# Adding x(t,c) and x(-t,-c) ahead of stage one in a fused Fourier mixing and gated feed-forward kernel

## The chip, the cores and the metric

The kernel runs on one core of one Trainium2 chip. The metric is the device time of one execution in microseconds. The kernel before took 616.23 us (median of three runs, 616.19 to 616.68).

The core has five engines, each with its own queue of instructions worked in order. PE (TensorE) multiplies matrices: it holds a weight tile of up to 128 rows by 128 columns and streams the other operand's columns through it into PSUM. ACT (ScalarE), DVE (VectorE) and POOL (GpSimd) work on tiles element by element. SP (SyncE) issues DMAs, which 16 DMA engines carry out.

## The reference

The input `x` has 8 batches of 3008 tokens and 256 channels. The kernel computes

```python
X = np.fft.fft(x, axis=1)            # over the 3008 tokens
X = np.fft.fft(X, axis=2).real       # over the 256 channels
g, val = X @ w_gate, X @ w_val       # 256 -> 1536
out = (0.5 * g * (1 + erf(g / sqrt(2)))) * val @ w_out   # 1536 -> 256
```

The real part of the two transforms is a sum over tokens t and channels c of x(t,c) times cos(2 pi (tk/3008 + cl/256)). The cosine is the same for (t,c) and (-t,-c), tokens counted modulo 3008 and channels modulo 256.

## The kernel before, in words

**Folding.** 3008 is 64 x 47. A token is 47 t1 + j; 64 values of t1 and two halves of j (j below 24, and j from 24 on; the 48th is a zero) lie on the 128 partitions, so a tile holds 24 values of j of 256 channels each. `load_x` (line 201) brings them into three tiles `xins`, eight j each. `fold_x` (218) adds and subtracts channel c and channel 256 - c and writes the two halves, 127 elements each, into `xf` as bf16; `singles` (213) copies channels 0 and 128. For batch 0 DVE folds, for the later ones POOL, two j in a call, in slots spread over the main loop two batches ahead (lines 1042 to 1051).

**Stage one** is the transform over t1. `a_step(b, k)` (486) makes two products of 256 columns, for two values of j, with weights `G[:, j, :]`, into a bank of `ps_d`; ACT (in batch 1 sometimes DVE) copies it to `S1`. Twelve such steps make 24 products a batch. `z_write` (505) sends `S1` to HBM, `z_read` (549) brings it back as `Ap` with 96 partitions: (j, and cosine or sine). Batch 0 takes another way: `a_group(J)` (513), six of them, uses the array in four column groups, and one DMA each goes from `S1` to `Ap` directly.

**Stage two** is the transform over j. `b_steps(b, eo, q)` (560) makes, for 32 frequencies and the two folded halves `eo`, a product with 128 columns of `Ap` as weights and 47 columns of a table (`TP`, `TQ`, for frequency 0 `T0P`, `T0Q`) as the other operand: 64 products a batch, eight in a bank. `evac_top` and `evac_rest` copy each bank to `Y`, 1505 frequencies long. `n_turn`, `n_step` and `n_read` prepare one more row from `Ap`, the table copy `TF` and `TB`.

**The feed-forward part** has the channel transform multiplied into its weights once (`gen_w`, line 411, with the tables `CW`, from weights that `load_w` fetches in parts of 256, 256, 512 and 512 columns and `cast_w` turns to bf16, mostly on POOL). A unit (`open_unit`, 647) is one block of 128 hidden channels and up to 512 frequencies; it gives rows for frequencies k and -k. There are 36 units in a batch, 288 in all, the first 12 of a batch with 481 frequencies. PE makes four or five products a unit into `ps_g` and `ps_v`; ACT applies the Gelu (`glp`, `glm`); DVE makes `ev`, `h` for k, and `dv`; POOL makes `h` for -k from `glm` and `dv` once for two units. In the units listed in `SPLIT` one PE product is replaced by work on DVE (`go`), POOL (`go` + `ge`) and ACT (Gelu of `go`, two units later). The second layer's products with `Wo_sb` go in eights at the end of a unit (`STEPS`) into `ps_o`; ACT copies to `osb`, SP stores.

**Order.** All orders are written out by hand: `_InOrder` keeps program order on each engine. The main loop (955 to 1074) runs over units; the tables `a_first`, `reads_first`, `plan`, `extra` say in which unit of a batch the next batch's stage-one and stage-two steps, the folds and the loads stand. `fill` puts stage-two products between a unit's own. In batch 0 the rest of the weights are made in units 0 to 7 (`extra`). `ps_g` has two banks, `ps_v` two tiles of two banks (each for two units), `ps_o` and `ps_d` one bank each. All loads and stores but two go through SP's queue, in order; the program gives DMAs eight semaphores in turn, so that a DMA may wait for the one eight before it.

**The start** (873 to 930) makes the tables with sines on ACT, folds and transforms batch 0, and keeps PE busy with `warm`, 25 products in all whose result nobody reads. `prow` is a row of numbers that `cols_t` turns into columns by products with one column each.

Of the kernel before, what the change touches and what calls it, by code (L numbers as in the profile page):

```python
# [10 lines left out]
BF16 = mybir.dt.bfloat16  # L11
AF = mybir.ActivationFunctionType
# [25 lines left out]
def kernel(  # L38
# [27 lines left out]
    NJ = 48  # L66
    HJ = 24
    KP = 96
# [14 lines left out]
    TP = const_pool.tile([128, 2 * N2], BF16)  # L83
    TQ = const_pool.tile([128, 2 * N2], BF16)
    T0P = const_pool.tile([128, NJ], BF16)
    T0Q = const_pool.tile([128, NJ], BF16)
# [17 lines left out]
    Ap = const_pool.tile([128, NG, C], BF16)  # L104
# [8 lines left out]
    col_b = const_pool.tile([128, 1], FP32)  # L113
    col_c = const_pool.tile([128, 1], FP32)
    col_j = const_pool.tile([128, 1], FP32)
    prow = const_pool.tile([1, 641], BF16)
    cols = const_pool.tile([128, 5], FP32)
    col_w = const_pool.tile([128, 1], FP32)
# [6 lines left out]
    def S1_tile():  # L125
        return work.tile([128, HJ, C], BF16, tag="S1", bufs=1, name="S1")

# [69 lines left out]
    def z_tile():  # L197
        return dram.tile([HJ, 128, C], BF16, tag="z", bufs=2, name="z")


    def load_x(b, i):
        xt = xins[i]
        for o, n, nh in ([(0, 7, 2), (7, 1, 1)] if i == 2 else [(0, 8, 2)]):
            src = ap_replace(
                x, ap=[[N2 * C, N1], [HJ * C, nh], [1, n * C]],
                offset=x.offset + (b * T + 8 * i + o) * C)
            p_step = xt[:, :, :].ap[0][0]
            dst = ap_replace(
                xt[:, :, :], ap=[[p_step * 2 // nh, N1 * nh], [1, n * C]],
                offset=xt[:, :, :].offset + o * C)  # L210
            sync.dma_start(out=dst, in_=src)

    def singles(i, a0=0, an=8):
        pool.tensor_copy(
            _sub(xf, [[C, an], [128, 2]], (8 * i + a0) * C),
            _sub(xins[i], [[C, an], [128, 2]], a0 * C))

    def fold_x(b, i, eng, a0=0, an=8, single=True):
        xt = xins[i]
        o0 = (8 * i + a0) * C  # L220
        lo = _sub(xt, [[C, an], [1, 127]], a0 * C + 1)
        hi = _sub(xt, [[C, an], [-1, 127]], a0 * C + 255)
        ea = _sub(xf, [[C, an], [1, 127]], o0 + 1)
        od = _sub(xf, [[C, an], [1, 127]], o0 + 129)
        eng.tensor_tensor(ea, lo, hi, op=ALU.add)
        eng.tensor_tensor(od, lo, hi, op=ALU.subtract)
        if single:
            singles(i, a0, an)
# [6 lines left out]
    vec.memset(xins[2][:, 7, :], 0.0)  # L235
# [6 lines left out]
    pool.tensor_scalar(rowk, rowk, 1.0 / 64.0, None, op0=ALU.mult)  # L242
# [4 lines left out]
    row = lambda i, pat, off=0: _sub(prow, pat, 128 * i + off, 0, 1)  # L247
    for k in range(2):
        iota(row(0, [[24, 4], [6, 2], [3, 2], [1, 3]], 12 * k), [[1, 4], [0, 2], [4, 2], [8, 3]], 24 * k, 0)
    for i, (base, sign) in enumerate(((0, 1), (0, 1), (1, -1))):  # L250
        iota(row(1 + i, [[12, 8], [6, 2], [1, 6]]), [[0, 8], [sign, 2], [0, 6]], base, 0)
    pool.memset(row(0, [[128, 4], [1, 32]], KP), 0.0)
    pool.memset(row(4, [[1, 129]]), 1.0)

    def cols_t():
        ps = ps_o()
        for i in range(5):
            pe.matmul(ps[:, i : i + 1], _sub(prow, [[1, 128]], 128 * i, 0, 1),
                      _sub(prow, [[1, 1]], 640, 0, 1), start=True, stop=True)
        vec.tensor_copy(cols, ps[:, :5])  # L260
        vec.tensor_scalar(col_j, cols[:, 0:1], 1.0 / N2, None, op0=ALU.mult)
        vec.tensor_scalar(col_w, cols[:, 4:5], -TWO_PI, None, op0=ALU.mult)

    def quats():
        for o, b0 in ((0, 0.25), (N2, 0.0)):
            pool.tensor_scalar(
                _sub(quat, [[1, N2]], o), _sub(cols, [[0, N2]], 1),
                0.25, b0, op0=ALU.mult, op1=ALU.add)
# [4 lines left out]
    def rows_t():  # L273
        pool.tensor_scalar(col_c, col_p, 1.0 / C, None, op0=ALU.mult)
# [6 lines left out]
        iota(_sub(rowt, [[NG, 2], [1, NG]], TG), [[0, 2], [-11, NG]], 0, 0)  # L281
# [20 lines left out]
    vec.memset(zero, 0.0)  # L302
    act.activation(col_m[:, :], zero[:, :], AF.Sin)

# [6 lines left out]
    vec.tensor_scalar(col_a, col_p, 360.0, None, op0=ALU.mult)  # L311
    vec.scalar_tensor_tensor(col_a, col_f, -719.0, col_a, op0=ALU.mult, op1=ALU.add)
    vec.tensor_scalar(rowj, rowj, col_a, None, op0=ALU.add)
    vec.scalar_tensor_tensor(col_b, col_f, -2.0, col_p, op0=ALU.mult, op1=ALU.add)
    vec.tensor_scalar(col_h[1], col_b, -TWO_PI, None, op0=ALU.mult)
    vec.tensor_scalar(col_h[0], col_b, TWO_PI, -TWO_PI, op0=ALU.mult, op1=ALU.add)
# [13 lines left out]
    def phase_g(i):  # L330
        ph, red = pha_g[i // 2][:, i % 2, :], red_g[i // 2][:, i % 2, :]
# [10 lines left out]
        vec.tensor_scalar(cos, cos, 0.25, None, op0=ALU.add)  # L342
        reduce_phase(ph, red)

    def sin_g(i):
        for h in range(2):
            act.activation(
                _sub(G, [[128, 8], [1, 64]], i * 8 * 128 + h * 64),
                _sub(reds[i], [[64, 8], [1, 64]], 0), AF.Sin, scale=col_h[h][:, :])

    def turn_g(odd):
        for to, of, n, sign in (((1, 33, 8, 1.0), (33, 1, 8, -1.0), (3, 35, 8, -1.0), (35, 3, 8, 1.0))
                                if odd else ((0, 0, 16, 1.0), (2, 2, 16, -1.0))):
            pat = [[128, 8], [64, 2], [4, n]]
            to, of = _sub(G, pat, 16 * 128 + to), _sub(G, pat, of)
            if odd:
                act.activation(to, of, AF.Copy, scale=sign)
            else:
                pool.tensor_scalar(to, of, sign, None, op0=ALU.mult)

# [8 lines left out]
    def sin_t(ph, red):  # L369
        s = lambda t, o, n: _sub(t, [[1, n]], o)  # L370
        act.activation(s(ph, 0, 2 * NJ), s(red, TO, 2 * NJ), AF.Sin, scale=col_w)
        for i, t in enumerate((TP, TQ)):
            act.activation(
                _sub(t, [[N2, 2], [1, N2]], 0), _sub(red, [[0, 2], [1, N2]], i * N2), AF.Sin, scale=col_w)
        act.activation(_sub(TB, [[1, 2 * NG]], 0), s(red, TG, 2 * NG), AF.Sin, scale=col_w)
        for i, t in enumerate((T0P, T0Q)):
            pool.tensor_scalar(
                t[:, :MID], s(ph, i * NJ, MID), cols[:, 3:4], None, op0=ALU.mult)
            pool.tensor_scalar(
                t[:, MID:], s(ph, i * NJ + MID, MID), cols[:, 2:3], None, op0=ALU.mult)  # L380
# [3 lines left out]
    def phase_c():  # L384
        both = red2_tile()
        redc.append(both)
        for q, (o, n) in enumerate(((0, 129), (129, 127))):
            act.activation(both[:, o : o + n], rowc[:, o : o + n], AF.Copy, scale=col_c[:, :],
                           bias=0.25 * (q + 1))

    def reduce_c():
        reduce_phase(redc[0][:, :C], redc[0][:, C : 2 * C])

    def sin_c():
        act.activation(_sub(CW, [[1, C]], 0), redc[0][:, C : 2 * C], AF.Sin, scale=-TWO_PI)
# [709 lines left out]
```

## Time and profile before

| | us | share |
|---|---|---|
| time of the profiled execution | 616.14 | |
| its span, first to last instruction | 614.30 | |
| PE matmul busy | 597.6 | 97% |
| DVE busy | 567.2 | 92% |
| POOL busy | 501.5 | 82% |
| ACT busy | 487.4 | 79% |
| a batch of the main loop (batches 1 to 5) | 72.3 to 72.4 | |
| granted PE clock, over the span | 1.00 | |

Busy time is the time in which an engine had at least one instruction at work. The products are pipelined: the mean of a group is from a product's start to its modelled end, longer than what it costs in a row of many; the cost is the distance between starts, which the chain shows as a time for so many products. The page's groups name the output and input tiles, the shapes, the count, the busy time, the mean in ns, and the idle time of the engine before them with what ended it. Nearly all instructions carry line 25, the helper that issues them, so tiles and shapes tell them apart.

### The profile page before, as it was taken

Reading aid. Unit: us, or ns where it says so; the run is one execution under the profiler, and the core shown is the slowest. Engines: PE = TensorE matmul, PEld = TensorE weight load, DVE = VectorE, ACT = ScalarE, POOL = GpSimd, SP = SyncE. Lnnn points to the kernel's source line nnn. Section 1 sums busy time; section 2 is a strip of 40 time slices with the busy share of each in tenths; the row PEclk is TensorE's granted clock in tenths of the full one; section 3 lists DMA queues with packets and bytes.
Section 4 is the critical chain, followed back from the end, with each engine's and each line's share of the span. In section 5 each row is a group of like instructions: output and inputs, shape, how many; then the busy total and the mean of one; then the engine's idle time right before and its main releaser. Section 6 shows DMA issues by size and latency. Waiting matters only on the chain.

```text
span 614.3 us, 13104 instructions
## 1 busy us (share of the span) xinstructions
PE 597.6 (97%) x4581; PEld 399.8 (65%) x4638; DVE 567.2 (92%) x689; ACT 487.4 (79%) x1011; POOL 501.5 (82%) x525
## 2 busy tenths in 40 slices
PE   4999999999999999999999999999999999999997
PEld 2556666666676666666667666766667666666666
DVE  8788999999999999999999999999999999999992
ACT  8798789877898787977789778887789878776762
POOL 5599999989999899798998899898997755665552
PEclk9999999999999999999999999999999999999999
DMA  7989424772257612674246633476223712222123
GB/s 277 348 233 264 135 65 116 202 216 60 61 149 197 197 39 70 205 224 113 66 120 173 192 93 74 121 207 209 46 67 100 203 37 52 59 47 52 39 48 86
DMA packets 63459, 80.79 MB, mean 132 GB/s; under 512 B 8186, under 2 KB 56826, under 8 KB 60674
## 3 DMA queue, kind: packets, MB, share of 16 engines
q1 hardware_dynamic: 61682, 79.05, 45.5%
q0 software_dynamic: 1552, 0.79, 0.9%
q8 instruction: 36, 0.59, 0.4%
q14 instruction: 29, 0.24, 0.1%
q10 hardware_dynamic: 160, 0.13, 0.1%
HBM read 43.47 MB, written 35.68 MB: 129 GB/s over the span
## 4 chain that ended last, share of the span: by engine, by line
PE 91%; ACT 3%; DMA 2%; DVE 2%; SPq 1%; issue 1%; ACTq 0%; POOL 0%
PE ps_o L25 38%; PE ps_g L25 26%; PE ps_v L25 20%; PE ps_d L25 7%; DMA xin<-in_x_dram 1%; ACT glm L25 1%; ACT osb L25 1%; ACT S L25 1%; SPq L850 1%; DMA out_dram<-osb 1%; ACT glp L25 0%; DVE h L25 0%; SPq L855 0%; DVE red L25 0%; DVE ev L25 0%
## 5 line engine op out<-in xcount | busy, mean ns | idle before, releaser
L25 POOL TENSOR_TENSOR h<-glm,dv 128x1024 bf16<-128x1024 bf16 (+1 forms) x138 | 290.8, 2109 | 80.6 <-DVE dv L25 60.0
L25 PE MATMUL ps_o<-Wo_sb,h 128*128 128x256 bf16 x2124 | 284.2, 272 | 1.0
L25 PEld LDWEIGHTS <-h 128*128 128x128 bf16 x2208 | 211.0, 98 | 58.3 <-issue 0.9
L25 DVE SCALAR_TENSOR_TENSOR ev<-nq,WN,ps_v 128x512 f32<-128x512 bf16 (+1 forms) x276 | 202.2, 734 | 23.4 <-PE ps_v L25 13.4
L25 ACT ACTIVATE glp<-ps_g 128x512 bf16<-128x512 f32 (+1 forms) x288 | 169.8, 590 | 37.2 <-PE ps_v L25 18.6
L25 ACT ACTIVATE glm<-ps_g 128x512 bf16<-128x512 f32 (+1 forms) x241 | 142.2, 590 | 56.6 <-PE ps_g L25 44.0
L25 DVE TENSOR_TENSOR h<-glp,ps_v 128x1024 bf16<-128x1024 bf16 (+2 forms) x150 | 173.0, 1154 | 4.2 <-ACT glp L25 3.5
L25 DVE SCALAR_TENSOR_TENSOR dv<-ev,ps_v 128x1024 f32<-128x1024 f32 (+1 forms) x138 | 164.9, 1195 | 0.0
L25 POOL TENSOR_TENSOR xf<-xin 128x254 bf16<-128x254 f32 x168 | 118.1, 724 | 0.4 <-PE ps_g L25 0.4
L25 PE MATMUL ps_v<-Y,WOP 128*128 128x512 bf16 (+1 forms) x288 | 107.7, 374 | 0.1
L25 PE MATMUL ps_v<-Y,WE 128*128 128x512 bf16 (+1 forms) x286 | 107.3, 375 | 0.0
L25 PE MATMUL ps_g<-Y,WE 128*128 128x512 bf16 (+1 forms) x266 | 99.3, 373 | 0.0
L25 PE MATMUL ps_g<-Y,WOP 128*128 128x512 bf16 (+1 forms) x257 | 96.0, 373 | 0.8
L25 PE MATMUL ps_g<-Y,WOM 128*128 128x512 bf16 (+1 forms) x241 | 90.3, 375 | 0.2
L25 PEld LDWEIGHTS <-WOP 128*128 128x128 bf16 x576 | 55.5, 97 | 49.2 <-ACT WOP L25 0.6
L25 PEld LDWEIGHTS <-WE 128*128 128x128 bf16 x576 | 56.0, 97 | 27.8 <-issue 2.0
L25 ACT ACTIVATE osb<-ps_o 128x512 f32<-128x512 f32 x92 | 54.2, 589 | 13.4 <-PE ps_o L25 11.9
L25 POOL TENSOR_TENSOR go<-go,ge 128x480 f32<-128x480 f32 (+1 forms) x47 | 58.1, 1236 | 7.1 <-DVE go L25 7.1
L25 PEld LDWEIGHTS <-Ap 96*128 96x128 bf16 (+1 forms) x561 | 39.6, 96 | 31.7 <-issue 0.2
L25 ACT ACTIVATE S<-ps_d 128x512 bf16<-128x512 f32 x82 | 48.9, 596 | 0.2 <-PE ps_d L25 0.2
L25 PEld LDWEIGHTS <-G 128*128 128x128 bf16 (+1 forms) x289 | 22.0, 110 | 26.5 <-issue 4.7
L25 DVE SCALAR_TENSOR_TENSOR go<-nq,WN,ps_g 128x480 f32<-128x480 bf16 (+1 forms) x47 | 34.3, 730 | 2.6 <-ACT glp L25 1.9
(134 smaller groups left out, 371.8 us busy)
## 6 DMA issues: line engine op xcount, KB each, us to landing
out_dram<-osb SPq DMA_DIRECT2D x358, 64.0 KB
xin<-in_x_dram SPq DMA_DIRECT2D x16, 1024.0 KB
Ap<-z SPq DMA_DIRECT2D x20, 512.0 KB
xin<-in_x_dram SPq DMA_DIRECT2D x8, 896.0 KB
z<-S SPq DMA_DIRECT2D x7, 768.0 KB
z<-S SPq DMA_DIRECT2D x6, 512.0 KB
nq<-nrow SPq DMA_DIRECT2D x8, 376.2 KB
z<-S SPq DMA_DIRECT2D x9, 256.0 KB
```

Of the source, the lines that this page charges most:

```text
L25: return lambda *a, **k: self._tc.keep_in_program_order(call(*a, **k))
L850: queues[q % 2].dma_start(out=rows_ap(rows[0][0], 32, rows[1][0] - rows[0][0], 2), in_=_sub(t, [[C, 2], [1, C]], 0, 32 * q, 32))
```

## The change

The pair x(t,c) + x(-t,-c) is added before stage one, so that stage one has 12 values of j instead of 24 for each half.

- For a reversed token the order of t1 turns round on the partitions, which a load alone would take in single rows. `flip(b)` copies the needed tokens of `x` within HBM to `xr`, reversed, in two DMAs of 11 x 64 and 12 x 64 rows of 1 KB. `flip(1)` stands between the second and third pair of weight loads, `flip(2)` in unit 4 of batch 0, the later ones at unit 24, three batches ahead.
- `load_x` becomes four DMAs (`put_x`), each to every second partition: two from `x`, two from `xr`. In batch 0 it is three, all from `x`.
- `fold_part` replaces `fold_x` on POOL, in halves of two j: the first adds channels 0 and 128 and adds the reversed partner to 254 channels of two j in place, in float32; the second folds as before. There are 12 halves a batch, with their own unit tables (`folds`), where there were 12 calls. Batch 1's stand in units 3 to 14 of batch 0 instead of 0 to 11.
- `a_step` uses the weights `GA`, made from `G` by `gen_ga` (two ACT instructions in unit 8 of batch 0), six steps of two products a batch, all in `ps_d` and copied by ACT; `z`, `S1` and `Ap` halve.
- In stage two, a column block of `Ap` serves two frequencies: 32 products of 94 columns, `TPQ` with three groups of 94 columns in place of four tables. `fill` puts one product at a time where it put two.
- Batch 0 isn't added ahead; `a_group` runs its six groups with 16 products of 128 columns each, keeping of each folded half only the cosine or sine part, so that its `Ap` has the new layout.
- At the start 12 rows of `prow` are made instead of five, ACT clears them first, and the phases of `G` and `CW` are reduced as integers with one bitwise and instead of two float32 operations. `gen_tf` has seven POOL instructions instead of three, in unit 17 instead of 13. `STEPS`, `SPLIT` and `warm` are as they were.

```diff
+    def flip(b):
+        xr[b] = xr_tile()
+        for s, (j0, n) in enumerate(((N2 - HP + 1, HP - 1), (HP, HP))):
+            d = xr[b][s, :, :, :]
+            sync.dma_start(
+                out=ap_replace(d, ap=[[C, n], [HP * C, N1], [1, C]], offset=d.offset),
+                in_=ap_replace(x, ap=[[C, n], [-N2 * C, N1], [1, C]],
+                               offset=x.offset + (b * T + N2 * (N1 - 1) + j0) * C))
...
+        put_x(i, 0, 0, 4, xb(j, [[C, 4]]))
+        put_x(i, 1, 0, 4, xb(N2 - HP - j, [[-C, 4]]))
+        put_x(i, 0, 5 - o, 3 + o, xv(0, HP - 2 + o - j, [[-C, 3 + o]]))
+        put_x(i, 1, 4, 4, xv(1, j, [[C, 4]]))
...
+    def fold_part(b, i, k):
+        a0 = k // 2 * 2
+        o0 = (HP * (b % 2) + 4 * i + a0) * C
+        at = lambda s, o, pat: _sub(xins[i], [[C, 2]] + pat, (s + a0) * C + o)
+        if k % 2 == 0:
+            pool.tensor_tensor(
+                _sub(xf, [[C, 2], [128, 2]], o0), at(0, 0, [[128, 2]]), at(4, 0, [[128, 2]]), op=ALU.add)
+            pool.tensor_tensor(
+                at(0, 1, [[128, 2], [1, 127]]), at(0, 1, [[128, 2], [1, 127]]),
+                at(4, 255, [[-128, 2], [-1, 127]]), op=ALU.add)
+        else:
+            for o, op in ((1, ALU.add), (129, ALU.subtract)):
+                pool.tensor_tensor(
+                    _sub(xf, [[C, 2], [1, 127]], o0 + o), at(0, 1, [[1, 127]]),
+                    at(0, 255, [[-1, 127]]), op=op)
...
+        ps = ps_d()
         for i in range(2):
-            jj = 2 * k + i
-            on_half(ps, pe.matmul(
-                ps[:, i * C : (i + 1) * C], G[:, jj, :], _sub(xf, [[1, C]], jj * C),
-                start=True, stop=True))
...
+            pe.matmul(
+                ps[:, i * C : (i + 1) * C], GA[:, 2 * k + i, :],
+                _sub(xf, [[1, C]], (HP * (b % 2) + 2 * k + i) * C), start=True, stop=True)
+        act.activation(_sub(S1, [[1, 2 * C]], 2 * k * C), ps, AF.Copy)
...
-                g = 8 * q + gi
+                g = 4 * q + gi
...
+                t = TPQ[0 if m1 else eo]
+                o = gi * TS
                 r = slice(0, 1) if m1 else slice(0, 128)
+                pat, off = ([[2 * TS, 2], [1, N2]], 0) if g == 0 else ([[TS, 2], [1, N2]], TS + 36 * g % N2)
+                keep(pe.matmul(ps[r, o : o + TS], w, _sub(t, pat, off, 0, KP), start=True, stop=True))
...
     def gen_tf():
-        for i, t in enumerate((TP, TQ, T0P)):
-            pool.tensor_copy(TF[:, i, :], t[:, :NJ])
+        for i, t in enumerate(TPQ):
+            pool.tensor_tensor(TF[:, i, :], t[:, 1, :NJ], t[:, 2, :NJ], op=ALU.add)
+        pool.tensor_copy(TF[:, 2, :], TPQ[0][:, 0, :NJ])
+        for k in range(4):
+            v = _sub(TB, [[1, GH]], k * GH)
+            pool.tensor_scalar(v, v, cols[:, 2 + k : 3 + k], None, op0=ALU.mult)
...
     for f0, n in ((256, 256), (512, 512)):
         for i in (1, 0):
             load_w(f0, i, n)
+        if n == 256:
+            flip(1)
+    pool.memset(xins[0][:, 4, :], 0.0)
     load_x(1, 0)
...
-    extra = {1: [lambda: cast_w(1024)], 2: [lambda: turn_g(False)], 13: [gen_tf]}
+    extra = {1: [lambda: cast_w(1024)], 2: [lambda: turn_g(False)], 8: [gen_ga], 17: [gen_tf]}
...
+    a_first = {9: 0, 10: 1, 11: 2, 12: 3, 14: 4, 16: 5}
+    a_later = {2 * k: k for k in range(HP // 2)}
+    folds = ((16, 18, 19, 21, 22, 24, 26, 27, 29, 30, 32, 34), (5, 7, 9, 11, 19, 21, 23, 25, 29, 31, 33, 35))
+    reads = ({12: 0, 15: 1, 18: 2}, {4: 0, 8: 1, 13: 2})
...
-        def fill(most=2):
+        def fill(most=1):
...
-                if i < 12:
-                    fold_x(1, i // 4, pool, i % 4 * 2, 2)
...
+                if 3 <= i < 15:
+                    fold_part(1, (i - 3) // 4, (i - 3) % 4)
+            if b + 2 < B and i in folds[b > 0]:
+                fold_part(b + 2, *divmod(folds[b > 0].index(i), 4))
```

More of the change, by code (lines that the diff above doesn't have):

```diff
@@ L67 @@
     HJ = 24
+    HP = HJ // 2
     KP = 96
@@ L949 @@
         for h in range(2):
[L950 to L952 removed]
+            later[i0 + h] = [(1, q, 2 * h, 2 * h + 2)]
+    first = {23: ["n"], 22: [(1, 0, 0, 4)]} | {
+        23 + q: [(1, q, 0, 4)] for q in range(1, 4)}
     plan = [first | evens, later | evens]
```

356 lines of the change are left out of this document (173 added, 183 removed).

## The prediction

> **What bounds the kernel now.** I read the page's engine totals, then the chain that ended last, then the busy time stage by stage, then the timeline around the waits. The totals and the chain:
>
> ```profile
> PE 597.6 (97%) x4581; PEld 399.8 (65%) x4638; DVE 567.2 (92%) x689; ACT 487.4 (79%) x1011; POOL 501.5 (82%) x525
> ...
> PE 91%; ACT 3%; DMA 2%; DVE 2%; SPq 1%; issue 1%; ACTq 0%; POOL 0%
> ```
>
> TensorE holds the end almost alone, so its time removed is time saved until DVE (92%) takes over. Batch 3, cut into units 0–11 (stage one of the next batch inside), 12–17 (neither) and 18–35 (stage two inside); columns are window, length, PE, PEld, DVE, ACT, POOL, clock, DMA share, GB/s:
>
> ```profile
> 242.80:266.90 24.10, 24.05 (x174) 16.86 (x174) 22.76 (x28) 21.10 (x41) 20.63 (x21) 1.00 0.64 183
> 266.90:279.10 12.20, 12.15 (x89) 7.97 (x89) 11.63 (x14) 9.22 (x16) 10.38 (x11) 1.00 0.66 201
> 279.10:315.60 36.50, 36.23 (x293) 24.36 (x297) 35.01 (x41) 29.24 (x67) 34.22 (x36) 1.00 0.32 84
> ```
>
> PE idles 0.37 of 72.80 us; DVE idles 1.34, 0.57 and 1.49: 3.4 in all. That is the room. How close DVE follows is in the timeline: `dv` ends, frees its bank of `ps_v`, and PE writes into it 0.26 us later (308.74 to 309.00).
>
> ```profile
> 307.52 1.22 DVE L25 SCALAR_TENSOR_TENSOR dv<-ev,ps_v 128x1024 f32<-128x1024 f32 x1
> 309.00 0.38 PE L25 MATMUL ps_v<-Y,WE 128*128 128x512 bf16 x1
> ```
>
> Batch 0 differs: from the first `h<-glm,dv` on, POOL is as full as PE (second line), and before it the DMAs are busy at 0.88 (first line).
>
> ```profile
> 27.90:54.80 26.90, 26.44 (x189) 14.81 (x191) 22.89 (x37) 24.21 (x49) 25.26 (x49) 1.00 0.88 252
> 54.80:103.80 49.00, 48.63 (x380) 32.23 (x384) 47.21 (x54) 39.85 (x88) 48.61 (x53) 1.00 0.48 137
> ```
>
> Prices: from the chain, 16 stage-two products and 8 of 256 columns; from the groups by form, the folds and POOL's f32 adds.
>
> ```profile
> 21.50 0.41 PE ps_g L25 x16
> 48.29 0.87 PE ps_o L25 x8
> L25 POOL TENSOR_TENSOR xf<-xin 128x254 bf16<-128x254 f32 x168 | 118.1, 724 | 0.4 <-PE ps_g L25 0.4
> L25 POOL CAST xf<-xin 128x4 bf16<-128x4 f32 x84 | 16.9, 202 | 0.0
> L25 POOL TENSOR_TENSOR go<-go,ge 128x512 f32<-128x512 f32 x22 | 28.0, 1272 | 0.0
> ```
>
> **The change part by part.** The sum is made against the profiled execution, 616.14 us (span 614.30 and 1.84 around it), 0.09 under the median of 616.23.
>
> Batches 1 to 6, PE. Stage one loses 12 of 24 products of 256 columns: 12 x 0.87/8 = 1.31 us a batch. Stage two goes from 64 products of 47 columns (0.41/16 = 0.026 each, 1.64) to 32 of 94. Their price lies between 0.026 and twice that; on the line through 0.026 at 47 and 0.109 at 256 columns it is 0.044, so 1.42: 0.2 saved (0 to 0.8). PE: 1.5 us a batch (1.3 to 2.1).
>
> By the Trainium skill (TensorE: Matmul & The Clock Gate, Back-to-back issue gap) a stream of weight loads and products of 128 columns keeps some 81 ns apiece, though alone a product takes N/2.4 + 2.5 ns. By the 81, stage two would cost about 2.6 us and the batch would gain only 0.35; by the other formula 94 columns take 42 ns. The chain's rows, each with its own weight load, agree with the second.
>
> Do DVE and POOL follow? DVE's work per batch stays at 69.4 of 72.8; it would have 71.3. Where PE waits on a bank freed only 0.26 us before, DVE's idle time is half its own echo. In units 0–11, 1.31 goes from PE and DVE has 1.34 to give. I take 1.3 a batch; bounds 0.5 (only a third of DVE's idle time is usable) and 2.1 (all of PE's). POOL: a fold pair was 2 x (two of 0.68, start to start, and a cast of 0.15) = 3.0; now a half A (4-element add 0.15, f32 add of 508 elements, by the 512-element `go` 1.22 apart) of 1.37 and a half B (two of 0.68) of 1.36: 16.4 instead of 18.1 a batch; it needs no more than it frees. ACT loses 6 copies `S<-ps_d` (0.596) and gains two small `Y` copies; off the path. Steady part: 6 x 1.3 = -7.8 (-3 to -12.6).
>
> Data. `z` halves; the flip adds 1.5 MB read and written a batch, each load becomes four. At unit 24 the flip stands on SP ahead of output stores and, through the rotating DMA semaphores, of the eighth DMA after it. `osb` has two buffers and a pair every 6 us, so a store may be some 6 us late; the cover is that spare buffer. Without it ACT's `osb` copy would wait, then `ps_o`. Nothing taken; up to +1 a batch in rival 3.
>
> The start, to 21 us. POOL writes 12 `prow` rows for 5 (0.43 each, +3.0), behind ACT's zeroing of 1408 elements (by 1.02 for 1024, about 1.3); `cols` and with it the second fold on DVE come up to 1.2 late. Against it: DVE drops three range reductions (2 x 0.69, 0.43), stage-two products fall from 99 to 51. The filler matmuls `warm` stay and cover part. +0.3 (-0.5 to +1.3).
>
> The flip of batch 1 is issued ahead of the 512-column weight loads.
>
> ```profile
> 24.04 1.04 POOL L25 CAST wb<-wst 128x1024 bf16<-128x1024 f32 x1 [1.51 <-DMA wst<-in_moe_w_val_dram]
> 28.43 0.38 PE L25 MATMUL ps_o<-wb,CW 128*128 128x512 bf16 x1
> q1 hardware_dynamic: 61682, 79.05, 45.5%
> ```
>
> The cast waits for its load already; its product comes 3.35 us after the cast's end. The flip's time: no row shows HBM to HBM. Lower end 1.5 MB at the 335 GB/s of the stretch 20 to 40 us, 4.5 us; upper end twice the mean rate's 5.3 us (79.05 MB in 45.5% of 16 engines' 614 us is 283 GB/s), as both sides are HBM: 10.6. I take 7, near the middle, since both rows have one HBM side. The load slips by 7, PE waits 7 - 3.35, less 0.4 because the last `Ap<-S` ahead of it is 128 KB smaller (at 335 GB/s): +3.3 (0.8 to 7). The loads of 1024 slip too, inside this.
>
> The Trainium skill (DMA: Bandwidth & Descriptors, Why a DMA increments its semaphore by 16 and not by 1) says that a copy runs on the largest number up to 16 that divides both sides' outermost counts; the flip's are 11 and 12. That is 128 packets in a row on some engines, about 7.4 us by the mean rate; no trace here shows such a split.
>
> Batch 0, PE and POOL. By unit 13 six stage-one steps (0.22 each) are gone or moved behind: -1.3. POOL then: up to the `go` add at 88.98 (unit 31) the new order holds 11 halves (15.0) where 8 pairs of 1.51 stood (12.1), because batch 1's folds start at unit 3 and batch 2's follow at 16; `gen_tf`, formerly done before 54.8, is now 7 instructions, about 1.9. That add comes 4.8 later.
>
> ```profile
> 88.98 1.26 POOL L25 TENSOR_TENSOR go<-go,ge 128x512 f32<-128x512 f32 x1
> 91.09 0.62 ACT L25 ACTIVATE glm<-go 128x512 bf16<-128x512 f32 x1
> ```
>
> ACT read it 0.85 after its end. ACT works in order: behind this Gelu stand `glm` and `glp` of the next units, which free `ps_g` for PE. So 4.8 - 0.85 = 3.9 late, less what ACT's gaps give back: +3.2 (0, if ACT's 9.2 idle us of 49 absorb it, to 4.8). PE doesn't regain it.
>
> Sum: 616.1 - 7.8 + 0.3 + 3.3 - 1.3 + 3.2 = 613.8 us.
>
> **Rivals.** (1) Batch 0 hides both: the flip runs at the lower end and POOL's lag stays inside ACT's gaps. For it: no wait on `go` in batch 0 costs anything now. Against: POOL has 0.4 us idle in 49. With all of PE's 1.5 a batch, 616.1 - 9 - 1.3 + 0.3 + 0.8 = 607. (2) DVE becomes the bound: 0.5 a batch; for it the 0.26 us, against it 3.4 us idle. 613.8 + 4.8 = 618.6. (3) Slower: the flip holds the weights back. One transfer, in units 2 to 7 of batch 0. With the rest as forecast it decides against the change from a wait of 5.6 us, a flip of 9.3; at its upper end 10.6 it waits 7 and gives 617.5; if flips at unit 24 cost 1 us in each of 5 batches too, 622. (4) The weight loads show: a load of `Ap` lasts 97 ns by its group, and if 94 columns don't hide it as the chain's rows say 47 do, 32 of them take 3.1 us and a batch gains nothing: 613.8 + 7.8 = 621.6; the row of 16 in 0.41 speaks against. (By the 81 ns of the Trainium skill's page named above, 0.35 a batch, it would be 619.5.) (5) It doesn't cut what it says: the built program has 84 products of 256 columns in stage one for 168 in the loop, 256 wide ones in stage two for 512, so this is all but excluded.
>
> **How the numbers follow.** Forecast 0.50, (1) 0.20, (2) 0.08, (3) 0.16, (4) 0.03, other mishaps 0.03. Around 613.8 the two batch-0 terms spread 610 to 617.5, the likeliest case's own range. Over all 606 to 619.5 leaves about 2 in 10 out. A difference of 0.2% (1.2 us) is about what can be told. Faster: 0.33 of the forecast's 0.50, 0.20 of (1), 0.03 elsewhere: 0.56. Same: 0.12 of the forecast, 0.02 elsewhere: 0.14. Slower: 0.30.
>
> **What would show it.** Right: `ps_d<-xf,GA` 84 times at 0.109 apart; 94-column products some 0.044 apart; batches 1 to 6 about 71.1 us each with DVE idle near 2; a wait of POOL's 1024-element cast on `wst` past 30 us and of PE behind it; ACT's `glm<-go` waiting for POOL in batch 0, at most 4 us. Wrong: a steady batch over 72 us (DVE or POOL bound), or no wait at all ahead of 104 us (then 607), or `osb` waiting for `out_dram` at each unit 24.

## The result, and the profile after

The changed kernel takes 620.74 us (median, 620.14 to 621.82) against 616.21: 1.0074 times as long, 95% interval 1.0057 to 1.0092. It is slower by 4.5 us; 613.8 was predicted, with a range of 606.0 to 619.5. The profiled execution took 620.70 us, its span 618.6, 4.3 over that of before.

The busy times by stage, cut at the second product of unit 0 (`ps_v<-Y,WOP`, which marks the start of a unit) and of units 36, 252 and 287: the start, batch 0, batches 1 to 6, batch 7, the end. First the kernel before, then the changed one; the columns are window, length, PE, PEld, DVE, ACT, POOL, clock, DMA share, GB/s.

```profile
0.00:24.75 24.75, 15.63 (x236) 9.85 (x238) 19.59 (x55) 19.07 (x48) 11.07 (x40) 1.00 0.87 291
24.75:97.97 73.22, 72.39 (x541) 44.46 (x548) 66.38 (x88) 61.76 (x132) 70.77 (x99) 1.00 0.63 184
97.97:531.88 433.91, 431.63 (x3262) 292.00 (x3303) 415.02 (x475) 356.47 (x744) 377.25 (x364) 1.00 0.46 128
```

```profile
0.00:29.36 29.36, 18.81 (x195) 10.10 (x197) 19.29 (x64) 18.52 (x49) 12.94 (x44) 1.00 0.74 232
29.36:108.24 78.88, 71.86 (x497) 42.98 (x504) 64.74 (x85) 61.93 (x134) 69.14 (x81) 1.00 0.68 203
108.24:536.21 427.97, 425.52 (x3004) 283.42 (x3039) 413.73 (x474) 342.08 (x720) 369.24 (x303) 1.00 0.44 122
```

The steady part gains 5.94 us, the start loses 4.61, batch 0 loses 5.66; batch 7 and the end together gain 0.05. In batch 0 PE is busy 0.5 us less and idle 7.0 instead of 0.8.

**The start.** The timeline of PE in the changed kernel, with the fillers `ps_d<-G`:

```profile
17.95 0.59 PE L26 MATMUL ps_d<-G 128*128 128x512 bf16 x1 [0.85 <-ACT S L26]
18.76 3.62 PE L26 MATMUL ps_d<-G 128*128 128x512 bf16 x8 [0.22 <-issue]
22.17 0.57 PE L26 MATMUL ps_g<-wb,CW 128*128 128x256 bf16 x2
23.23 2.97 PE L26 MATMUL ps_d<-G 128*128 128x512 bf16 x13
26.04 0.34 PE L26 MATMUL ps_v<-tab,Ap 96*128 96x94 bf16 x4
```

Eight products of 512 columns last 3.62 us here, and 4.5 us later thirteen of them last 2.97: they start 0.427 and 0.216 us apart. In the kernel before nine took 2.33:

```profile
14.75 2.33 PE L25 MATMUL ps_d<-G 128*128 128x512 bf16 x9
```

PE's array runs at half rate until about 22.4 us; before, it had reached the full rate by 15.2. The folds come late as well: DVE's first at 8.34 for 6.47, the last ends at 16.55 for 13.83.

**Batch 0.** The waits of PE in its timeline, then the rows of POOL and of SP's queue around the third and the fourth:

```profile
38.93 0.59 PE L26 MATMUL ps_o<-wb,CW 128*128 128x512 bf16 x2 [1.11 <-POOL wb L26]
49.10 0.39 PE L26 MATMUL ps_d<-xf,GA 128*128 128x256 bf16 x2 [0.59 <-ACT GA L26]
64.18 0.38 PE L26 MATMUL ps_d<-xf,GA 128*128 128x256 bf16 x2 [2.12 <-POOL xf L26]
77.27 0.21 PE L26 MATMUL ps_d<-tab,Ap 96*128 96x94 bf16 x2 [1.74 <-issue]
```

```profile
60.61 2.15 POOL L26 TENSOR_TENSOR h<-glm,dv 128x1024 bf16<-128x1024 bf16 x1 [2.56 <-DVE dv L26]
62.72 1.40 POOL L26 TENSOR_TENSOR xf<-xin 128x254 bf16<-128x254 f32 x2
```

```profile
70.03 1.27 SPq L26 DMA_DIRECT2D xin<-in_x_dram  x2
71.35 1.27 SPq L26 DMA_DIRECT2D xin<-xr  x2
72.66 0.59 SPq L26 DMA_DIRECT2D Ap<-z  x1
```

The first wait is for the weights of 1024 columns on. Their load stands on SP behind a load that waits for the copy; the chain shows the copy's second DMA and then this load:

```profile
21.48 8.57 DMA xr<-in_x_dram
30.66 7.12 DMA wst<-in_moe_w_val_dram
```

At 64.18 PE waits for the last half fold of batch 1, which stands on POOL behind an `h` that itself waited 2.56 us for DVE. At 77.27 it waits for the last third of `Ap`, whose read stands on SP behind four loads of `x`.

**The steady part.** Batch 3 of the changed kernel, units 0–11, 12–17 and 18–35, and two groups by form:

```profile
251.21:274.17 22.96, 22.91 (x162) 15.70 (x162) 22.50 (x28) 18.42 (x36) 19.70 (x17) 1.00 0.52 145
274.17:286.46 12.29, 12.24 (x84) 7.87 (x84) 11.69 (x14) 9.10 (x16) 10.65 (x10) 1.00 0.54 158
286.46:322.88 36.42, 36.20 (x265) 24.20 (x268) 35.06 (x41) 29.59 (x69) 33.36 (x29) 1.00 0.43 124
```

```profile
L26 PE MATMUL ps_d<-xf,GA 128*128 128x256 bf16 x84 | 16.0, 272 | 2.7 <-POOL xf L26 2.1 <-ACT GA L26 0.6
L26 PE MATMUL ps_d<-tab,Ap 96*128 96x94 bf16 x228 | 43.2, 206 | 2.2 <-issue 1.7
```

DVE idles 0.46 us in units 0–11, where it idled 1.34. Products of 94 columns start 0.042 us apart. PE idles little in these rows, yet by the starts of its products against their prices it waits, in the mean of batches 1, 3 and 5, 0.09, 0.16 and 0.15 us in units 0, 6 and 12 ahead of a product into `ps_v` (0.01 or less before the change); in batches 2, 4 and 6 it is 0.26, 0.20 and 0.15 (0.04 or less before). Such a wait is shorter than the modelled end of a product and so does not show as idle.

### The profile page after: what moved, and what is told of

Same layout as the page of the kernel before. It is cut to its first block, busy times and chain, and to the rows that moved or that the text cites. A ratio compares the mean times of both kernels' runs of the same rounds, so it can differ in the third digit from the quotient of the medians.

```text
span 618.6 us, 12413 instructions
## 1 busy us (share of the span) xinstructions
PE 594.2 (96%) x4238; PEld 390.1 (63%) x4289; DVE 564.1 (91%) x695; ACT 472.7 (76%) x989; POOL 493.8 (80%) x450
## 4 chain that ended last, share of the span: by engine, by line
PE 83%; DMA 5%; DVE 3%; POOL 3%; ACT 2%; issue 2%; SPq 2%; ACTq 0%; DVEq 0%; POOLq 0%
PE ps_o L26 36%; PE ps_g L26 25%; PE ps_v L26 18%; PE ps_d L26 4%; DMA xr<-in_x_dram 1%; POOL h L26 1%; DMA xin<-in_x_dram 1%; SPq L26 1%; DMA wst<-in_moe_w_val_dram 1%; DVE h L26 1%; DVE dv L26 1%; POOL xf L26 1%; ACT osb L26 1%; DMA xin<-xr 1%; DMA z<-S 1%
## 5 line engine op out<-in xcount | busy, mean ns | idle before, releaser
L26 PE MATMUL ps_g<-Y,WOP 128*128 128x512 bf16 (+1 forms) x271 | 101.3, 374 | 1.4
L26 PE MATMUL ps_g<-Y,WE 128*128 128x512 bf16 (+1 forms) x258 | 96.3, 373 | 0.5 <-ACT glm L26 0.5
L26 POOL TENSOR_TENSOR xf<-xin 128x254 bf16<-128x254 f32 (+1 forms) x126 | 68.6, 562 | 0.4
L26 POOL TENSOR_TENSOR xin<-xin 128x508 f32<-128x508 f32 x42 | 53.4, 1271 | 0.0
L26 PE MATMUL ps_d<-tab,Ap 96*128 96x94 bf16 (+2 forms) x246 | 43.6, 204 | 2.2 <-issue 1.7
L26 ACT ACTIVATE Y<-ps_d 128x192 bf16<-128x192 f32 (+5 forms) x156 | 38.7, 380 | 0.3 <-PE ps_d L26 0.3
```

The source lines that it names most:

```text
L26: return lambda *a, **k: self._tc.keep_in_program_order(call(*a, **k))
```

## The experiments

Edits are against the changed kernel or the one named. Times are medians, ratios those to the kernel before. "Unit 0" is its start as defined above. Unit 0, batch lengths and all lines are those of the one profiled execution of a kernel, which lies up to 3.3 us from the median where a kernel's times scatter.

### The start: clock or loads

`warm_early`:

```diff
     for i in (1, 0):
         load_w(0, i, 256)
+    ps = ps_d()
+    for _ in range(24):
+        pe.matmul(ps, _sub(zero, [[0, 128]], 0), _sub(zero, [[0, 512]], 0), start=True, stop=True)
```

> 24 products of 512 columns of a tile of zeros are put ahead of everything else on PE, from about 1.2 us. In the changed kernel the filler products between 18.8 and 22.2 us start 0.427 us apart, and those from 23.2 us on 0.216 apart. Theory A (PE's own clock: less work in the start leaves the array at half rate until 22 us): the fillers then stand 0.216 apart from the first on, the first product of the channel weights (22.17) comes near 20.3, unit 0 some 2 us earlier, the time near 618.5. Theory B (the late loads alone set the start, the slow fillers only fill a wait): unit 0 stays within 0.5 us of 29.4 and the time at 620.7.

622.04 us, 1.0096 (1.0066 to 1.0125). Unit 0 starts 1.1 us earlier, at 28.28, in a profiled execution of 620.11 us, the second shortest of six (619.55 to 624.93); the median does not follow. The rate rises between 6.7 and 7.0 us (products from 0.427 to 0.219 apart) and is lost again; the windows show it:

```profile
12.00:14.00 2.00, 0.96 (x32) 0.79 (x32) 1.71 (x4) 0.08 (x1) 1.77 (x4) 0.92 1.05 326
14.00:16.00 2.00, 1.55 (x31) 0.68 (x23) 2.00 (x6) 1.30 (x4) 0.75 (x2) 0.50 0.46 100
```

Between 10.9 and 13.5 us PE mostly waits for folds. So neither A nor B as written: the fillers were still slow when they ran. `clock_fill` has the 24 products of `warm_early` and fills that stretch too. (These added products are "the fillers" from here on, those of `warm` the old ones.)

```diff
...
-        if n == 1:
-            warm(2)
+        if n in (1, 3):
+            warm((6, 2)[n // 2])
...
-    warm(WF[0])
+    warm(WF[0], bank=ps_g)
```

> As warm_early, where PE's clock rose at 6.7 us (products of zeros from 0.427 to 0.219 us apart) and had fallen again by 13.8, after a stretch in which PE waited for the folds. Now six fillers instead of two stand behind group 1, two more behind group 3, and the ten behind group 5 go to a bank of ps_g, so that they need not wait for ACT's copies of ps_d. Theory A2 (the clock falls because the halved products of stage one leave PE idle between the folds): fillers stand 0.216 apart from 7 us on, the first product of the channel weights comes at 19.2 to 19.6 (the cast ahead of it ends at 19.2) instead of 22.17, and unit 0 starts at 26.4 to 27; batch 0 then gives some of it back, since the wait at 76.6 to 77.3 us comes at a fixed time in all runs so far: 618 to 619. Rival: the clock falls all the same (more fillers only push the work back): unit 0 at 28.3 or later.

```profile
11.05 1.47 PE L26 MATMUL ps_d<-G 128*128 128x512 bf16 x6
16.49 2.33 PE L26 MATMUL ps_g<-G 128*128 128x512 bf16 x10
18.66 0.38 PE L26 MATMUL ps_g<-wb,CW 128*128 128x256 bf16 x2
```

A2 holds for the start: ten fillers in 2.33 us, the channel weights 3.5 us earlier, unit 0 at 25.67 instead of 29.36. So between these two executions 3.7 of the start's 4.6 us are the clock; 0.9 is left. The time is not the 618 to 619 forecast but 622.2 us, 1.0089 (1.0066 to 1.0112), in ten executions from 619.29 to 625.46. The profiled one is the longest of them, and its batch 0 takes 87.31. PE's largest waits there, what the cast waited for, and a window after the second wait:

```profile
33.14 0.59 PE L26 MATMUL ps_o<-wb,CW 128*128 128x512 bf16 x2 [3.62 <-POOL wb L26]
36.33 1.06 PE L26 MATMUL ps_o<-wb,CW 128*128 128x512 bf16 x2
```

```profile
32.04 1.04 POOL L26 CAST wb<-wst 128x1024 bf16<-128x1024 f32 x1 [9.14 <-DMA wst<-in_moe_w_val_dram]
```

```profile
80.00:82.00 2.00, 2.00 (x10) 1.09 (x8) 0.14 (x1) 1.15 (x6) 2.00 (x3) 0.50 0.00 0
```

The wait that the prediction put down to the copy is now there, 3.62 us for the 512 column weights. And a wait of this size costs twice: after it, and after one of 3.56 us in unit 21, PE runs at half rate for 3 and 6 us.

`asc_first` and `act_queue` ask why the first loads are late.

```diff
-            put_x(i, 1, 4, 4, xb(N2 - HP - j, [[-C, 4]]))
-            put_x(i, 1, 1 - o, 3 + o, xb(N2 - 1 + o - j, [[-C, 3 + o]]))
+            put_x(i, 1, 4, 4, xb(N2 - HP - j - 3, [[C, 4]]))
+            put_x(i, 1, 1 - o, 3 + o, xb(N2 - 3 - j, [[C, 3 + o]]))
```

> The reversed half of batch 0 is read in ascending order of tokens, so that four rows of 1 KB lie side by side; the tokens are then the wrong ones for the reversed half, and nothing else differs. Theory B (the first loads are late because of their rows of 1 KB in descending order): the first fold starts near 6.6 us instead of 8.34, as in the kernel before (6.47), the folds end 1.5 to 2 us earlier and unit 0 starts 1.5 to 2 us earlier: near 619. Rival C (they are late because nine issues of 0.65 us stand on SP's queue where four stood): the first fold stays within 0.4 us of 8.34 and the time within 0.5 us of 620.7. Theory A (clock) says nothing of the loads; if PE is still cold, less than the full gain arrives.

```diff
...
-            put_x(i, 1, 4, 4, xb(N2 - HP - j, [[-C, 4]]))
+            put_x(i, 1, 4, 4, xb(N2 - HP - j, [[-C, 4]]), act if i else sync)
```

> Two of batch 0's nine loads, one each of parts 1 and 2, are issued on ACT's queue ahead of its first table load, so that SP issues seven. Theory C (issues on SP's queue space the loads): the last fold ends 1 to 1.3 us earlier than 16.55, near 15.4, though ACT's phases and G come 1.2 later; unit 0 up to 1 us earlier. Rival H (the rate of the DMA engines with these rows of 1 KB): the last fold stays at 16.3 to 16.6 and the first fold comes later than 8.3, because the early data now stand ahead of part 0's; time 620 to 622.

DVE's folds with ascending rows:

```profile
6.98 2.44 DVE L26 TENSOR_TENSOR xf<-xin 128x1016 bf16<-128x1016 f32 x3 [0.49 <-DMA xin<-in_x_dram]
11.13 2.46 DVE L26 TENSOR_TENSOR xf<-xin 128x1016 bf16<-128x1016 f32 x3 [1.11 <-DMA xin<-in_x_dram]
13.90 2.65 DVE L26 TENSOR_TENSOR xf<-xin 128x508 bf16<-128x508 f32 x6 [0.32 <-DMA xin<-in_x_dram]
```

The first fold comes 1.4 us earlier, the last ends at 16.55 all the same, and the time is 620.12 (1.0056). PE's rate rises no sooner for it: products of 512 columns still start 0.427 us apart at 23.4. With fewer issues on SP the first comes at 8.38 and the last ends at 16.37: 622.6 us (1.0094). So the descending rows explain part 0's delay and neither explains the later parts. What holds these back stays open; by the difference of the two starts above it is worth at most 0.9 us.

### Batch 0: which wait, and what stands behind it

`no_flip`: `flip` is not called, and `xv` in `load_x` reads `x`.

```diff
         xv = lambda s, k, pat: ap_replace(
-            xr[b][s, :, :, :], ap=[[HP * C, N1]] + pat + [[1, C]],
-            offset=xr[b][s, :, :, :].offset + k * C)
+            x, ap=[[N2 * C, N1]] + pat + [[1, C]], offset=x.offset + (b * T + HP * s + k) * C)
...
```

> No copy in HBM is made: the loads of batches 1 to 7 read unreversed rows of x itself where they read the copy, in the same shapes; so the reversed tokens are wrong ones, and 10.5 MB of reading and writing and fourteen issues on SP are gone. The prediction's flip term (the 512 column weights late, PE waiting): PE's waits ahead of 48 us go (1.1 us), and the time falls by 1 to 1.5 us, to about 619.4. Rival F (the flips cost in every batch, through SP's queue and the DMA engines): also 0.3 to 1 us in each of batches 1 to 4, near 616 to 618. Rival G (the flip is hidden anyway): within 0.5 us of 620.7.

620.72 us, 1.0065 (1.0043 to 1.0088): rival G by the time. PE's wait for the weights goes, and unit 4 is 1.3 us shorter; the waits in units 15 and 21 stay (1.90 and 2.35). Behind the second PE falls to half rate, which it did not in the profiled execution of the changed kernel, and unit 21 is 2.0 us longer. So this time does not show that the copy costs nothing.

`fold_early` (first line) and `fold_z` (both):

```diff
-                if 3 <= i < 15:
-                    fold_part(1, (i - 3) // 4, (i - 3) % 4)
+                if 2 <= i < 14:
+                    fold_part(1, (i - 2) // 4, (i - 2) % 4)
...
-            loads = (0, 14, 19) if b else (8, 12, 18)
+            loads = (0, 14, 19) if b else (8, 12, 20)
```

> The twelve half folds of batch 1 stand in units 2 to 13 of batch 0 instead of 3 to 14, so that the last half comes ahead of POOL's first h instead of behind it. Theory D (PE's waits of 2.12 us at 64.2 and of 1.74 us at 77.3 both come from that last half: the first directly, the second because z and Ap of batch 1 follow from it): both go and the time falls by 3.5 to 3.9 us, to about 617. Theory D2 (the second wait is SP's: the read of the last third of Ap stands behind four loads of x on its queue): only the first goes, about 618.6. Rival E (POOL's total is too large in batch 0): the wait comes back at another h or go, and the time stays within 0.6 us of 620.7.

> As fold_early, and in batch 0 the last load of x for batch 2 stands in unit 20 instead of 18, so behind the read of the last third of Ap on SP's queue. Theory D2 (PE's wait in unit 21 is for that read, which stands behind four loads of x; fold_early's gain of 2 us was lost there, where its wait grew from 1.7 to 4.2): the wait in unit 21 falls to under 0.5 us, batch 0 takes 75 to 76 us instead of 78.9, and the time is 616.5 to 617.5. Rival E2 (the DMA engines are full in this stretch, the order on the queue is nothing): the wait in unit 21 stays over 2 us, the time over 619.

`fold_early` takes 622.42 us (1.0093, 1.007 to 1.0115). The wait for the fold is gone and the one for `Ap` has grown to 4.16 us, ending at 76.92 instead of 77.27:

```profile
76.92 0.24 PE L26 MATMUL ps_d<-tab,Ap 96*128 96x94 bf16 x2 [4.16 <-issue]
```

None of the three expectations: the 2.1 us saved are waited away there, 2.4 more than before, and behind a wait of this length PE runs at half rate until some 81 us (a clock of 0.50 in the windows from 76 to 80 us). With the load of `x` behind the read of `Ap`, `fold_z` has no wait in unit 21, batch 0 takes 76.75 us, and the time is 618.36 (1.0032, 1.0015 to 1.005), 0.9 above the range forecast. D2 is right on the cause; 1.31 us come back one unit later, where PE waits for POOL's `NA`, the product of `Ap` and `TB`.

### The steady part

`ev_short`:

```diff
+        if r["kd"] and r["c0"] == 1024 and r["k"]:
+            return
...
-                d["dv"][:, :, :nm], d["ev"][:, :, :nm], 2.0, d["pv"][:, :, :nm],
-                op0=ALU.mult, op1=ALU.subtract))
+                d["dv"][:, :, :nm], _sub(d["ev"][:, :, :], [[512 * (r["c0"] != 1024), 2], [1, nm]], 0),
+                2.0, d["pv"][:, :, :nm], op0=ALU.mult, op1=ALU.subtract))
```

> In the first 12 units of each batch after the first, DVE's ev of every second unit is left out and dv takes the other unit's ev twice, so part of the output is wrong: DVE has 6 x 0.7 = 4.2 us less to do in each of those stretches and PE the same. Theory J (what the steady part fell short by, 1.0 us a batch for the 1.3 forecast, is PE waiting 0.09, 0.16 and 0.15 us in units 0, 6 and 12 for DVE to free ps_v): these waits go and a batch takes 0.3 to 0.45 us less than 71.0 and 71.9, in all 2 to 2.7 us less: 618.2. Rival K (these are waits for something else, or PE's 1.3 was overestimated): a batch within 0.1 us of 71.0 and 71.9.

Units 0–11 of batch 3:

```profile
253.13:275.94 22.81, 22.81 (x162) 15.70 (x161) 18.84 (x22) 18.43 (x36) 19.71 (x17) 1.00 0.52 146
```

DVE has 3.7 us less, PE the same products. The odd batches take 71.5 us, the even ones 70.1 to 70.5 (71.7 to 72.0 and 70.5 to 71.0 in the changed kernel), 2.3 less in all, and 617.5 us is measured. (The profiled execution is the longest of ten, 620.69; its batch 0, which has the same work as before, takes 82.36.) The waits in units 0 and 6 are gone, the one in unit 12 stays at 0.15. So J holds for two of its three waits: DVE keeps PE from at least 0.4 us a batch.

### Copy and clock together

`fill_late` is `clock_fill` with `flip(1)` and the loads of batch 1 behind all weight loads; `moved_cold` has that order, the edits of `fold_z`, `gen_ga` in unit 7 and `gen_tf` in unit 13, without the fillers; `all_moved` is `moved_cold` with the fillers and `WF = (10, 7)`, that is 7 instead of 13 of the old fillers ahead of stage two. The diff is the move of the copy.

```diff
...
-        if n == 256:
-            flip(1)
-    pool.memset(xins[0][:, 4, :], 0.0)
-    load_x(1, 0)
     for i in (1, 0):
         load_w(1024, i)
+    flip(1)
+    pool.memset(xins[0][:, 4, :], 0.0)
+    load_x(1, 0)
     load_x(1, 1)
```

> As clock_fill (unit 0 at 25.7 us, then PE waiting 3.62 us in unit 2 for the cast of the 512 column weights, which land behind the copy, and after that wait four products of 512 columns at 0.427 us apart), with the copy for batch 1 and its loads moved behind all weight loads on SP. Theory L (copy and late start cover each other: with the late start the copy's delay was free, with the early start it is PE's): unit 2 falls from 6.17 to 2.5 us and units 3 and 4 to their usual 2.1 and 2.0, no product at half rate; the waits at units 15 and 21 stay. About 622.2 - 5, near 617. Rival M (DMA engines are full whatever the order, the copy only moves): the wait turns up again at the folds of batch 1 and unit 15 or 21 grows by over 3 us; 620 or more.

> All moves of order in batch 0 without the fillers: the copy for batch 1 and its loads behind the weights, the half folds a unit earlier, the last load of x for batch 2 in unit 20, GA made in unit 7, the small tables of gen_tf in unit 13 instead of 17. PE's clock in the start is left as it is, so unit 0 stays at 28.3 to 29.8 us. If batch 0's loss is made of the waits named (1.1 to 1.4 for the weights, 0.7 for GA, 2.1 for the fold, 1.7 for Ap, 0.6 for go), batch 0 takes 72 to 73 us, against 78.9 in the changed kernel and 73.2 in the one before, and the time is 613.5 to 615. Rival M: over 617.

> moved_cold and the fillers of clock_fill together, with 7 instead of 13 fillers ahead of stage two in the start. Unit 0 at 24.3 to 25.7 us, batch 0 in 72 to 73.5, the steady batches as they are (71.0 and 71.9): 609.5 to 611.5, 1% below the kernel before. By rival M the early start is lost again in batch 0: over 613.

624.61 us (1.0121), 619.01 (1.0043) and 618.18 (1.0031). Unit 2 is down to 2.5 us in `fill_late`, so the weights were the copy's victim; but rival M is right on the time in all three, and the forecasts without it are missed by 4 to 8 us. In `all_moved` unit 0 starts at 24.79, as early as before the change, and batch 0 takes 80.81. POOL's timeline says why:

```profile
42.66 0.22 POOL L26 TENSOR_TENSOR xf<-xin 128x4 bf16<-128x4 f32 x1 [9.73 <-PE ps_g L26]
```

POOL has nothing to do from 32.9 on, because batch 1's rows are still being copied and loaded; the loads from the copy leave SP at 32.29 and 37.47. (The releaser that the view names had long been done.) PE, needing the folds, waits 2.37 us in unit 9, and the windows of 44 to 50 us show a clock of 0.93, 0.50 and 0.72.

`flip_first` issues the whole copy of batch 1 in the start, `flip_split` its first half, the second behind the 512 column weights. Both have the fillers, folds, `GA` and `gen_tf` of `all_moved` and the loads for batch 2 in units 11, 14, 20. `no_copy_moved` and `no_copy_cold` are the same without copies, with the reads of `no_flip`; the first has the fillers, the second has not, and keeps 13 of the old ones ahead of stage two where the other three have 7. The diff is the order of copy and loads in `flip_split`.

```diff
...
     for i in (1, 0):
         load_w(0, i, 256)
+    flip(1, (0,))
...
-        if n == 256:
-            flip(1)
-    pool.memset(xins[0][:, 4, :], 0.0)
-    load_x(1, 0)
+    flip(1, (1,))
     for i in (1, 0):
         load_w(1024, i)
+    pool.memset(xins[0][:, 4, :], 0.0)
+    load_x(1, 0)
...
```

> As all_moved, with the copy for batch 1 issued in the start, at about 8.5 us, right behind the first two weight loads, the loads of batch 1 back between the weight loads, and the loads of x for batch 2 in units 11, 14 and 20 of batch 0. Theory N (batch 0 is set by the row copy, loads, folds, stage one of batch 1, whose copy took from 21.8 to about 37 us on SP's queue in all_moved, so that POOL's first fold began at 42.7 after 9.7 us of waiting): between 9 and 20 us the DMA engines have room (a share of 0.33 to 0.56 from 14 to 20 us in the changed kernel), the first fold starts at 32 to 35 us, the waits of units 9 and 11 go (2.7 and 2.4 us) and the time falls to 610 to 613. Rival O (the DMA engines' total up to 45 us is the limit, wherever the copy stands): the copy delays the first part of Ap or the weights by what it gives, and the time stays within 1.5 us of 618.2.

> All moves of order and the fillers as in flip_first, with no copies at all: the reversed tokens are read as unreversed rows of x, so the output is wrong. What is left against flip_first is what the seven copies cost with an early start. Theory N: 609 to 611, flip_first at most 2 us above it, since its copy is covered. Rival O: flip_first 4 us or more above it. If even this one stays over 616, neither the copy nor its place sets batch 0, but POOL's and DVE's work.

> As flip_first, with only the first of the two copies of batch 1 in the start; the second stands behind the 512 column weights, ahead of the 1024 column ones, and all loads of batch 1 behind these. In flip_first PE waited 2.90 us for Ap, which stood behind the whole copy; in no_copy_moved it did not wait, and unit 0 came 3.4 us earlier. Theory N (copy and start collide on the DMA engines for as long as the copy's bytes take): with half of the copy early, unit 0 comes at 24.4 to 25.5 us instead of 27.8, batch 0 takes 74 to 75.5, and the time is 611.5 to 613.5, 0.5% below the kernel before. If the second half then holds the weights or the folds (rival O), batch 0 takes over 76 and the time stays near 615.5.

> no_copy_moved (610.9 us) without the fillers that keep PE's clock up, and with 13 fillers ahead of stage two as in the changed kernel; output wrong in the same way. It measures the clock's price where nothing in batch 0 covers a late start: theory A gives unit 0 at 28.2 to 29.5 us instead of 24.3 and a time of 614.5 to 616; if the late start is still covered, as moved_cold (619.0) and all_moved (618.2) suggest for the kernels with the copy, under 612.

| | us | ratio (95%) | unit 0 | batch 0 |
|---|---|---|---|---|
| `flip_first` | 615.48 | 0.9987 (0.9977 to 0.9997) | 27.79 | 73.94 |
| `flip_split` | 613.29 | 0.9946 (0.9934 to 0.9959) | 24.64 | 76.46 |
| `no_copy_moved` | 610.90 | 0.9916 (0.9903 to 0.9929) | 24.33 | 74.30 |
| `no_copy_cold` | 614.72 | 0.9972 (0.9961 to 0.9983) | 28.65 | 73.93 |

In `flip_first` the stage-two products of the start wait for `Ap` behind the copy:

```profile
24.46 0.33 PE L26 MATMUL ps_v<-tab,Ap 96*128 96x94 bf16 x4 [2.90 <-DMA Ap<-S]
```

Theory N holds where no copy is made: `no_copy_moved` comes as forecast, with batch 0 in 74 us; so batch 0 had been set by the copy and its place, and perhaps by the loads, which are moved as well. For `flip_first` it does not: at 615.48 instead of 610 to 613 that kernel lies 4.6 us above `no_copy_moved`, which was rival O's sign, because the copy now delays `Ap`. `flip_split` comes as forecast in time and in unit 0, but its batch 0 stays over 76. There PE waits 0.70 us in unit 11 for POOL's fold of the late rows, and 1.49 in unit 21 for `Ap`; that the second wait too comes from the late rows is inferred. The later copies cost nothing: batches 1 to 6 take the same time in `flip_first` and `no_copy_moved`, within 0.1 us in all.

Without the fillers the kernel without copies takes 3.8 us longer (614.72 against 610.90). Not all of this is the clock. The six more of the old fillers in `no_copy_cold` run right ahead of stage two, and at 0.216 us each they take 1.3; some 2.5 are left for the clock. Where a copy covers the start, fillers and `WF` together gain only 0.8 (619.01 to 618.18), which the intervals do not tell from nothing.

`flip_split`, which leaves nothing out, beats both kernels, the one before by 0.5%.

## Why the prediction was wrong

The sum, term by term, against the profiled executions:

| step | predicted | measured |
|---|---|---|
| batches 1 to 6 | -7.8 | -5.9 |
| the start | +0.3 | +4.6 |
| copy ahead of the weights (units 3, 4) | +3.3 | +1.1 |
| stage-one steps gone or moved (units 5, 8, 12, 14, 16) | -1.3 | -1.4 |
| POOL late in batch 0: last half fold (unit 15), `go` (unit 33) | +3.2 | +2.3, +0.7 |
| `GA` (unit 9) | not costed | +1.0 |
| read of `Ap` behind loads of `x` (unit 21) | not costed | +1.9 |
| | -2.3 | +4.3 |

The terms of batch 0 are the lengths of its units against the same units before.

- **The start** is the step that failed. It was taken at +0.3, between -0.5 and +1.3, and measured +4.6, the only term outside its own bounds. The working counted rows on POOL, reductions on DVE and products on PE, and took "the filler matmuls `warm` stay and cover part". They covered nothing, because they ran at half rate themselves. With the rate kept up (`clock_fill`) unit 0 comes 3.7 us earlier, over half of the 6.6 us by which the sum missed. These 3.7 are a difference of two executions; as unit 0 scatters from 28.2 to 30.0 us at the old fillers, it could be 2.5 to 4.3. The rate came up late because PE waited between folds: this is shown in so far as filling the waits, on top of an early rise, kept it up. That PE waited because the groups of stage one are halved in columns is argued; `asc_first`, where the first fold came earlier and the rate did not, speaks for it. The other 0.9 goes with loads that are late, for a reason that stays open.
- **The copy** was right as a mechanism, and its 7 us were somewhat low but inside their bounds of 4.5 to 10.6: the chain shows 8.57 us for its second DMA. Its price was wrong because the steps were added. A start that is 4.6 us later needs the weights 4.6 us later, so of 3.3 only 1.1 was left, and at the 1024 column weights. With the start brought forward alone, the copy's delay appears at the weights (3.62 us in `clock_fill`).
- **POOL late** was right in its sum, 3.0 of 3.2, and in part by luck. PE met POOL first at a product of stage one, whose last half fold it held. That fold was late through its place in the order and not through POOL's total: POOL had just stood idle 2.56 us, and with the fold a unit earlier PE's wait was gone (`fold_early`). The `go` add, which was to cost all of it, cost 0.7.
- **Two waits were not in the sum.** ACT makes `GA` in unit 8, directly ahead of the first product that needs it: 1.0. The working said that each load becomes four, but took nothing for the DMA that stands behind them on SP, the read of `Ap`: 1.9.
- **The steady part** gains 5.9 for 7.8. PE's products became cheaper by what was said (1.31 and about 0.2 us a batch), and DVE took 0.4 to 0.6 of it, in waits of 0.1 to 0.3 us in units 0, 6 and 12. Rival 2 is right in kind; the 1.0 a batch that is left lies between its 0.5 and the 1.3 taken. Rival 4 falls, as the products of 94 columns start 0.042 us apart. By the Trainium skill (TensorE: Matmul & The Clock Gate, Back-to-back issue gap) 94 columns at N/2.4 + 2.5 ns would take an estimated 42 ns; the trace agrees, and the page's 81 ns for a stream of weight loads and products of 128 columns is not what these rows follow.
- Of the rivals, (3) ends on the measured side and for a related reason: the copy is too long for its cover. In the changed kernel that is 1.1 us at the weights. With an early start it shows in full, and where depends on the order: at the weights (`clock_fill`), at batch 1's rows (`all_moved`) or at `Ap` (`flip_first`). The flips at unit 24 cost nothing, and no `osb` waited there.

## What to carry to other kernels

When several steps of a start or a first batch come late, their delays do not add: each hides the next, so a single fix may show nothing, or make it worse, until the chain behind it is moved as well. Price a cut of PE work ahead of the loop also by what it does to PE's rate, and read the rate from the distance of equal products. For a transfer that a new step waits for, follow the whole row of the queue behind it, and place it where the DMA engines have room.

## What the runs showed of the hardware

The rate of PE fell without a long idle stretch. In `warm_early` it was full from 7.0 us and half again by 13.8, with no gap between the starts of products longer than 1.45 us in between. Six more fillers kept it up in `clock_fill`; with the same fillers it fell again near 12 us in `all_moved`, where four of them lasted 1.91 us. Nor does the length of one wait decide. After waits of 2.22 to 2.37 us PE ran at half rate in `act_queue`, `ev_short`, `no_flip` and `all_moved`; after 2.12 us in the changed kernel and 2.90 us in the start of `flip_first` it did not. The Trainium skill (TensorE: Matmul & The Clock Gate, Part 1: The HAM clock gate) has the half clock return after an idle window of about 3.4 us; the runs agree on the two rates (0.427 and 0.216 us for 512 columns), and here waiting with products in between was enough. Products of zeros raise the rate as others do (`warm_early`, from 0.427 to 0.219 us). The scatter of the times goes with it: in `warm_early` executions of 619.55 and 620.11 us had a granted clock of 0.994, those of 621.97 to 623.82 one of 0.989, that of 624.93 one of 0.986.

The clock in the profile's rows is blind at the start. Of the changed kernel, where eight products took 3.62 us:

```profile
18.00:20.00 2.00, 1.78 (x4) 0.67 (x5) 1.35 (x5) 1.97 (x9) 0.88 (x3) 1.00 0.33 82
```

It says 1.00, where `warm_early`, at the same spacing of products, has 0.50. All rows seen with 0.50 lie behind a first rise of the rate.

The start itself scatters: unit 0 begins between 28.2 and 30.0 us in the nine kernels that leave PE's fillers of the start alone, the changed one among them, as the rate rises anywhere from about 20 to 24 us. Each of these starts is from one execution, that of the kernel before (24.75) too.
